# A sine on a constant: from the last place of ScalarE's order to its first

## The chip, the cores and the metric

The kernel runs on 1 core of one Trainium2 chip. The metric is device time in microseconds (us) of one execution. Three runs of the kernel before took 228.07, 229.65 and 228.75 us; their median, 228.75, is the time before.

Engines are named as in the profile: PE is TensorE, DVE is VectorE, ACT is ScalarE, POOL is GpSimd, SP is SyncE. "L591" is line 591 of the kernel's file.

## The reference

An attention with sketched features feeds a mixing block. There are 4 batches, 4 heads, 1088 tokens, head dimension 32, and 8 rows in each sketch; the model dimension is 128.

```python
def phi(x):                                   # 8 x 8 = 64 features
    a = np.einsum('rd,bhsd->bhsr', S1, x)
    b = np.einsum('rd,bhsd->bhsr', S2, x)
    return np.einsum('bhsi,bhsj->bhsij', a, b).reshape(*x.shape[:-1], r * r)
q_p, k_p = (phi(q), phi(k))
kv = np.einsum('bhsf,bhsd->bhfd', k_p, v)
z = np.sum(k_p, axis=2)
attn = np.einsum('bhsf,bhfd->bhsd', q_p, kv) / (np.einsum('bhsf,bhf->bhs', q_p, z)[..., None] + 1e-06)
x = attn.transpose(0, 2, 1, 3).reshape(B, S, H * D)      # (4, 1088, 128)
theta = x @ w_theta
zr, zi = x * np.cos(theta), x * np.sin(theta)
y = np.einsum('ts,bsd->btd', w_tok_r, zr) + np.einsum('ts,bsd->btd', w_tok_i, zi)
u = x + y
out = u + np.maximum(u @ w_ch, 0.0)
```

The token mixing, two 1088 x 1088 matrices on four batches, is the largest part of the work.

## The kernel before

**A list of operations with a written order.** The program doesn't issue instructions as it goes through its loops. It calls `op(engine, duration, function, writes, reads)` for each step, which notes the step in a list with the steps that it depends on; the engine is a letter (P for PE, V for DVE, A for ACT, G for POOL, S for SP), and the duration is used only where orders are planned. Then three tables written into the file decide the rest: `SEQUENCE` is the order in which all 1024 steps are issued, `PLACES` gives each of the 419 buffers its slot (a stretch of SBUF of a class such as "big" or "zs", or a PSUM bank), and `FILLS` puts 6 filler matmuls ahead of one small transpose (L418). Each engine works through its own steps in that order. Where two buffers share a slot, the first writer of the later one waits for the last reader of the earlier one, so a change in `PLACES` alone can make or remove waits.

**The opening.** POOL clears a small tile (L368), PE runs 11 filler matmuls and then the 6 of `FILLS` on it (both L366), DVE writes the constants (L347 to L361), among them `halfpi`, a column with pi/2 (L348), which the cosine takes as its bias (L1048). SP loads the two sketches into `st` (L381, L382), after DVE has cleared it (L388); ACT and DVE turn their words into fp32 (L395, L407), and PE transposes two maxima (L418). In the meantime k and q come in (L611, L649).

**The weights.** All inputs come as 8-byte words. `w_tok` is cut into 17 blocks of 128 x 1088 words, numbered 0 to 16. For each, `weight()` has SP load the words into a "zs" slot (L587); ACT makes the upper words into fp32 with a Prelu (L591, in two halves) and copies the lower words' bits into a "big" slot, the "step" (L594); DVE shifts the first (L315), and the sum of both is made either by a DVE instruction (L311) or, for the blocks 3, 5, 7 and 9 to 16, by a transfer that POOL issues and that adds into its target (`join`, L325). SP's next load of `w_tok` waits until ACT has read the words in the slot that it takes.

**Attention and angles.** Per batch, PE makes products of features and values, DVE their numerators and ACT copies them between (L986, L1091, L1100). `theta_stage` (L1019) has PE compute theta (L331) and turn x (L1035) for three chunks at a time; ACT rounds (L1044), DVE takes the difference (L318), ACT takes its absolute value (L1047), then the cosine as a sine with the bias `halfpi` (L1048) and the sine (L1050); DVE multiplies with x (L311).

**Mixing.** Batches are taken in the pairs (0, 1) and (2, 3), with fewer large products than the plain sum has. Many are sums of PE products over blocks of `w_tok` (L331), with POOL transfers or DVE making sums of the blocks themselves. `early_products` (L1302) copies a first product out of PSUM on ACT (L1314), which frees the bank for PE's next one; `carried` (L1324) scales it (L1333) and adds it back by POOL transfers. The last steps are the channel mix, the maximum, and the output transfers from SP.

**The sine on a constant.** The kernel's fourth step (L371) computes a sine of `halfpi` into a tile `warm` that nothing reads. In `SEQUENCE` it stands at the end of ACT's order. ACT's functions come in tables that an instruction loads (ACT_TABLE_LOAD in the profile); these loads aren't written in the kernel's file, they are put in when it is built, where a function needs another table than the one before it.

Of the kernel before, what the change touches and what calls it, by code (L numbers as in the profile page):

```python
# [17 lines left out]
AF = mybir.ActivationFunctionType  # L18
# [28 lines left out]
    0, 4, 5, 6, 2, 1, 7, 8, 10, 11, 9, 30, 89, 49, 95, 101, 31, 12, 13, 35, 52, 53, 90, 76, 50, 14, 15, 233, 20,  # L47
    91, 92, 102, 51, 290, 55, 56, 57, 58, 214, 54, 34, 59, 60, 77, 16, 96, 93, 236, 61, 62, 63, 64, 65, 66, 67,
    68, 78, 238, 17, 182, 36, 69, 215, 70, 71, 185, 239, 159, 187, 72, 73, 241, 242, 183, 184, 237, 240, 74, 33,
    160, 161, 131, 75, 80, 81, 26, 37, 134, 294, 27, 28, 132, 136, 234, 235, 300, 21, 82, 83, 292, 79, 295, 291,  # L50
    293, 296, 97, 98, 99, 29, 163, 84, 164, 139, 140, 243, 141, 210, 162, 301, 85, 86, 220, 221, 124, 133, 125,
    87, 142, 143, 175, 144, 244, 176, 103, 245, 104, 297, 216, 177, 88, 217, 135, 105, 18, 190, 191, 138, 19,
    178, 22, 145, 246, 322, 192, 193, 194, 302, 303, 427, 247, 109, 428, 325, 211, 137, 298, 299, 188, 304, 324,
    431, 432, 423, 424, 425, 212, 248, 305, 429, 430, 426, 186, 195, 433, 434, 435, 196, 169, 170, 118, 197,
    198, 213, 165, 166, 306, 323, 42, 44, 249, 250, 108, 251, 307, 334, 252, 253, 254, 255, 310, 311, 146, 147,
    148, 149, 436, 189, 167, 437, 326, 335, 226, 308, 227, 150, 151, 438, 439, 309, 312, 256, 152, 257, 258,
    153, 119, 154, 259, 440, 171, 43, 45, 32, 336, 23, 260, 155, 156, 157, 94, 100, 106, 337, 222, 441, 442, 46,
    199, 200, 201, 47, 48, 346, 348, 443, 202, 203, 204, 347, 107, 349, 110, 364, 444, 205, 206, 269, 445, 158,
    270, 366, 207, 313, 208, 448, 449, 446, 447, 365, 24, 209, 38, 452, 265, 111, 453, 454, 266, 228, 267, 455,
    268, 456, 112, 229, 459, 350, 172, 223, 271, 457, 179, 261, 458, 460, 272, 462, 475, 340, 341, 40, 352, 342,  # L60
    327, 450, 273, 477, 173, 274, 275, 338, 368, 276, 382, 168, 174, 277, 343, 351, 451, 467, 354, 478, 461,
    180, 367, 369, 353, 113, 355, 469, 470, 677, 385, 476, 673, 230, 463, 471, 181, 678, 679, 356, 328, 680,
    329, 278, 472, 224, 357, 262, 344, 473, 283, 464, 345, 468, 41, 669, 670, 671, 672, 674, 675, 676, 114, 115,
    339, 474, 492, 218, 681, 465, 466, 483, 314, 682, 683, 479, 481, 358, 263, 684, 282, 685, 480, 485, 486,
    219, 225, 360, 686, 316, 605, 264, 361, 494, 315, 482, 359, 120, 330, 284, 496, 287, 231, 687, 688, 370,
    371, 121, 317, 487, 318, 484, 319, 495, 285, 489, 689, 690, 691, 694, 705, 692, 698, 488, 320, 116, 695,
    232, 373, 394, 497, 525, 279, 693, 491, 490, 372, 529, 530, 531, 532, 521, 522, 523, 524, 122, 526, 527,
    528, 332, 696, 697, 39, 117, 331, 533, 534, 535, 536, 537, 708, 709, 288, 538, 396, 286, 699, 700, 706, 25,
    707, 539, 540, 541, 397, 126, 127, 128, 602, 701, 702, 499, 710, 711, 542, 557, 395, 333, 703, 704, 412,
    415, 384, 607, 713, 715, 123, 543, 129, 130, 721, 716, 560, 723, 604, 280, 561, 558, 559, 413, 493, 281,  # L70
    546, 547, 544, 545, 289, 550, 714, 717, 724, 321, 383, 603, 562, 563, 548, 549, 600, 553, 722, 554, 386,
    414, 416, 387, 718, 729, 731, 719, 720, 823, 824, 362, 551, 363, 388, 827, 828, 829, 552, 555, 725, 831,
    832, 833, 727, 400, 726, 728, 398, 399, 825, 830, 417, 556, 564, 374, 375, 391, 739, 834, 826, 740, 835,
    732, 565, 390, 389, 392, 393, 733, 734, 401, 735, 743, 738, 584, 606, 836, 837, 730, 838, 736, 376, 377,
    498, 576, 578, 579, 742, 585, 402, 839, 840, 841, 842, 567, 378, 737, 741, 575, 744, 380, 580, 500, 501,
    745, 746, 502, 843, 844, 418, 587, 588, 506, 504, 747, 629, 748, 752, 750, 577, 849, 847, 505, 404, 379,
    755, 848, 569, 845, 751, 846, 509, 582, 586, 381, 503, 581, 403, 589, 749, 590, 570, 419, 566, 405, 850,
    851, 591, 593, 592, 583, 596, 571, 572, 573, 599, 595, 420, 852, 421, 631, 598, 422, 853, 601, 854, 855,
    856, 857, 568, 507, 753, 612, 611, 406, 624, 613, 574, 594, 597, 610, 407, 756, 408, 410, 626, 770, 409,
    869, 871, 872, 614, 619, 646, 860, 862, 873, 609, 615, 874, 608, 878, 411, 510, 875, 617, 616, 508, 653,  # L80
    618, 645, 649, 623, 754, 712, 858, 868, 620, 511, 870, 863, 651, 880, 881, 876, 882, 884, 888, 647, 512,
    627, 656, 758, 877, 879, 859, 861, 655, 625, 652, 893, 635, 621, 622, 634, 769, 864, 866, 757, 767, 771,
    785, 778, 883, 886, 772, 768, 891, 650, 885, 777, 628, 774, 865, 867, 636, 887, 779, 633, 889, 931, 787,
    788, 637, 638, 639, 890, 897, 640, 641, 632, 643, 784, 780, 892, 648, 644, 630, 898, 773, 903, 654, 789,
    657, 659, 915, 775, 917, 786, 759, 658, 782, 660, 642, 760, 513, 900, 916, 761, 776, 514, 904, 515, 516,
    762, 790, 783, 792, 791, 805, 804, 914, 930, 806, 793, 795, 920, 929, 919, 896, 794, 796, 895, 800, 901,
    797, 661, 908, 662, 899, 909, 808, 963, 911, 807, 801, 802, 924, 798, 918, 902, 985, 811, 781, 913, 3, 810,
    907, 905, 812, 809, 814, 906, 813, 984, 965, 517, 518, 519, 932, 938, 520, 665, 666, 925, 663, 962, 667,
    819, 923, 799, 934, 763, 820, 821, 910, 935, 936, 912, 803, 960, 922, 921, 939, 926, 894, 927, 955, 937,
    933, 961, 940, 964, 967, 764, 928, 941, 765, 957, 952, 953, 942, 943, 946, 956, 966, 944, 822, 947, 948,  # L90
    959, 954, 958, 968, 998, 815, 668, 766, 986, 983, 969, 664, 949, 816, 817, 951, 989, 971, 973, 945, 950,
    970, 994, 972, 988, 818, 995, 978, 979, 980, 990, 981, 974, 975, 987, 1000, 976, 992, 999, 1004, 977, 982,
    1009, 1003, 1001, 1006, 1012, 1013, 991, 1008, 1014, 1015, 1007, 1002, 1005, 1011, 993, 997, 996, 1010,
    1020, 1021, 1022, 1023, 1016, 1017, 1018, 1019,
# [3 lines left out]
    46, 57, 47, 45, 60, 49, 56, 46, 54, 53, 47, 57, 57, 39, 61, 50, 34, 58, 40, 56, 50, 35, 59, 41, 61, 48, 36,  # L98
    52, 45, 62, 48, 60, 59, 44, 62, 46, 36, 56, 42, 57, 49, 37, 62, 43, 59, 54, 38, 45, 53, 31, 12, 16, 55, 58,
    41, 52, 9, 61, 62, 15, 62, 44, 62, 37, 60, 41, 61, 34, 55, 40, 62, 35, 54, 51, 30, 7, 19, 58, 55, 39, 51,  # L100
    14, 56, 61, 60, 42, 57, 36, 57, 39, 60, 35, 60, 40, 56, 34, 29, 49, 29, 5, 10, 58, 59, 44, 50, 5, 60, 53,
    54, 51, 46, 47, 49, 62, 52, 45, 60, 46, 57, 47, 49, 51, 53, 52, 59, 53, 45, 56, 48, 51, 62, 41, 62, 60, 56,
    32, 60, 61, 57, 33, 61, 62, 57, 28, 56, 60, 59, 32, 18, 22, 17, 19, 25, 1, 0, 24, 2, 10, 22, 12, 8, 25, 4,
    16, 23, 1, 4, 26, 14, 6, 26, 21, 2, 23, 21, 7, 23, 11, 9, 24, 7, 1, 26, 14, 12, 26, 11, 21, 24, 5, 5, 26,
    11, 17, 23, 3, 3, 26, 11, 27, 61, 62, 57, 20, 50, 13, 22, 38, 34, 59, 56, 61, 35, 36, 57, 58, 57, 38, 36,
    55, 58, 56, 20, 61, 61, 37, 59, 56, 38, 60, 57, 37, 55, 58, 31, 55, 41, 58, 39, 27, 62, 56, 61, 17, 50, 20,
    24, 36, 34, 60, 56, 56, 36, 38, 56, 62, 56, 34, 38, 60, 56, 59, 1, 59, 57, 38, 44, 61, 61, 36, 39, 60, 59,
    35, 40, 57, 60, 55, 58, 28, 62, 43, 60, 41, 27, 58, 57, 55, 17, 53, 15, 25, 36, 35, 59, 56, 59, 34, 36, 57,
    61, 56, 38, 35, 56, 61, 57, 11, 61, 61, 35, 60, 57, 37, 60, 57, 34, 62, 56, 30, 57, 40, 60, 39, 56, 62, 62,
    44, 56, 42, 60, 58, 57, 40, 58, 40, 27, 59, 62, 61, 5, 46, 14, 23, 23, 34, 34, 37, 59, 57, 60, 61, 5, 61,  # L110
    59, 37, 39, 55, 61, 34, 42, 59, 61, 35, 43, 26, 59, 61, 33, 57, 55, 57, 44, 60, 42, 58, 62, 57, 39, 60, 41,
    56, 55, 61, 62, 43, 58, 44, 59, 42,
)
FILLS = (
    (11, 6),
)


class Buf:


    def __init__(self, cls, shape, dt, name):
# [11 lines left out]
class Layout:  # L134
# [11 lines left out]
    def op(self, eng, dur, fn, w=(), r=(), acc=(), hold=(), lk=0, kind=0, mode=0, n=1, fly=0.0):  # L146
        o = Op()
# [11 lines left out]
        for x in r:  # L159
            b, key = parts(x)  # L160
# [1352 lines left out]
```

## Time and profile before

| what | value |
|---|---|
| runs | 228.07, 229.65, 228.75 us; median 228.75 |
| the profiled execution's own time | 229.23 us |
| its span, first to last instruction | 227.4 us (1.83 us of its time lie around the span) |
| mean granted clock of TensorE | 0.992 |
| ACT_TABLE_LOAD | 2 times, 1.28 us each: before the first L395 and before the first L1048 |
| sines L1048 | 12 times, 0.60 to 0.68 us |
| transfers of w_tok | 17, of 1088 KB, median 9.6 us from issue to landing |
| POOL's transfers that add | 44 of L325, 4.1 to 16.4 us from issue to landing |

A line of the timeline has the start in us, the duration in us, the engine, the line, the operation, the tiles (output<-input) with their shape, and how many instructions are put together; in brackets stands how long the engine was idle before and what ended that wait. In the chain of work, followed back from the last instruction, a line is one piece with its start, its length, and what it was. The windows give the busy time of each engine in a stretch.

### The profile page before, as it was taken

The numbers are of one execution on the slowest core, as the hardware profiler recorded it, in microseconds if no ns is written. First come the engines' busy times: TensorE is split into PE (matmuls) and PEld (weight loads), VectorE is DVE, ScalarE is ACT, GpSimd is POOL, SyncE is SP. The second block draws the span as 40 slices with busy tenths as digits, with TensorE's granted clock in tenths as the row PEclk, the third lists the DMA queues.
The fourth block names the chain that finished last, engine by engine and source line by source line (L and its number), as shares of the span: only waits on it lengthen the run. The fifth ranks groups of instructions, "written<-read, shape, count | busy, mean of one in ns | idle before, by whom it ended". The sixth has DMA issues, their size and how long they took to land.

```text
span 227.4 us, 4055 instructions
## 1 busy us (share of the span) xinstructions
PE 217.8 (96%) x1486; PEld 182.2 (80%) x1486; DVE 171.0 (75%) x388; ACT 126.1 (55%) x260; POOL 55.2 (24%) x92
## 2 busy tenths in 40 slices
PE   7999999998979999899989999999999999999993
PEld 3898999976867886588868788888888888888882
DVE  2799999999999989789997917985483663504763
ACT  2988798999999997999997545730000000000000
POOL 1067960001116300013322361968000000000000
PEclk9999999999979999999999999999999999999999
DMA  4999999994999999299999899999973000331442
GB/s 130 421 420 312 383 353 417 419 425 147 246 299 188 299 257 273 89 291 242 275 243 207 255 191 167 176 191 194 198 128 52 0 0 3 62 58 23 69 74 58
DMA packets 28888, 46.80 MB, mean 206 GB/s; under 512 B 18757, under 2 KB 19013, under 8 KB 26693
## 3 DMA queue, kind: packets, MB, share of 16 engines
q1 hardware_dynamic: 22532, 30.30, 39.0%
q0 software_dynamic: 6336, 16.26, 37.3%
q8 instruction: 11, 0.18, 0.3%
q14 instruction: 9, 0.07, 0.1%
HBM read 28.07 MB, written 2.23 MB: 133 GB/s over the span
## 4 chain that ended last, share of the span: by engine, by line
PE 54%; DVE 24%; DMA 10%; ACT 7%; issue 3%; POOL 0%; SPq 0%; DVEq 0%; ACTq 0%; POOLq 0%
PE ps L331 49%; DMA big<-big 5%; DVE big L311 5%; DMA zs<-w_tok 4%; DVE g L311 3%; DVE sm L318 2%; PE ps L366 2%; DVE hf L315 2%; DVE big L315 2%; DVE sm L311 2%; ACT big L591 2%; PE ps L1035 1%; DVE sm L315 1%; DVE lv L311 1%; PE ps L1087 1%
## 5 line engine op out<-in xcount | busy, mean ns | idle before, releaser
L331 PE MATMUL ps<-big,zs 128*128 128x288 f32 (+2 forms) x498 | 116.2, 387 | 2.2 <-DVE zs L311 1.4
L331 PEld LDWEIGHTS ps<-big,zs 128*128 128x128 f32 x498 | 91.2, 191 | 20.5 <-DVE zs L311 1.5
L325 POOL DMA_DIRECT2D big<-big x35 | 33.5, 1347 | 89.9 <-DVE big L315 29.7
L591 ACT ACTIVATE big<-zs 128x544 f32<-128x544 f32 (+1 forms) x33 | 23.3, 727 | 0.7 <-DMA zs<-w_tok 0.7
L594 ACT ACTIVATE big<-zs 128x1088 int32<-128x1088 uint32 (+1 forms) x18 | 21.4, 1190 | 3.1 <-DMA big<-big 1.7
L318 DVE SCALAR_TENSOR_TENSOR big<-ps,even,big 128x288 f32<-128x288 f32 (+2 forms) x23 | 10.5, 483 | 16.1 <-PE ps L331 15.8
L331 PE MATMUL ps<-mf,big 128*128 128x96 f32 x72 | 14.5, 295 | 0.1
L311 DVE TENSOR_TENSOR zs<-ps,g 128x768 f32<-128x768 f32 (+2 forms) x20 | 12.5, 630 | 2.1 <-ACT g L1050 1.7
L315 DVE TENSOR_SCALAR big<-big 128x1088 int32<-128x1088 int32 x17 | 12.2, 725 | 1.3 <-ACT big L591 1.1
L331 PEld LDWEIGHTS <-hf 128*128 128x128 f16 (+1 forms) x144 | 11.9, 105 | 1.2 <-issue 0.8
L311 DVE TENSOR_TENSOR big<-big,ps 128x288 f32<-128x288 f32 (+1 forms) x12 | 5.1, 433 | 9.9 <-PE ps L331 9.8
L311 DVE TENSOR_TENSOR g<-lv 128x768 f32<-128x768 f32 x12 | 11.2, 952 | 1.4 <-PE ps L1087 1.2
L331 PE MATMUL ps<-w,big 128*128 128x128 f32 (+1 forms) x76 | 12.2, 299 | 0.0
L331 PEld LDWEIGHTS ps<-w,big 128*128 128x128 f32 x76 | 10.7, 202 | 1.8 <-PE ps L331 0.6
L318 DVE SCALAR_TENSOR_TENSOR big<-ps,big 128x288 f32<-128x288 f32 (+1 forms) x15 | 6.5, 434 | 6.6 <-PE ps L331 6.5
L331 PEld LDWEIGHTS ps<-mf,big 128*128 128x128 f32 x72 | 10.9, 191 | 0.4 <-issue 0.4
L311 DVE TENSOR_TENSOR big<-big,hf 128x1152 f32<-128x1152 f32 x8 | 11.0, 1385 | 0.0
L325 POOL DMA_DIRECT2D big<-hf x9 | 10.3, 1300 | 2.8 <-DVE sm L315 2.0
L331 PE MATMUL ps<-mv,hf 128*128 128x96 f16 x108 | 10.8, 206 | 0.1
L331 PE MATMUL ps<-big,big 128*128 128x128 f32 x72 | 10.9, 279 | 0.0
L331 PE MATMUL ps<-sbk,g 128*128 128x64 f32 x72 | 9.5, 272 | 0.0
L331 PEld LDWEIGHTS ps<-big,big 128*128 128x128 f32 x72 | 9.3, 192 | 0.1
(195 smaller groups left out, 381.0 us busy)
## 6 DMA issues: line engine op xcount, KB each, us to landing
zs<-w_tok SPq DMA_DIRECT2D x17, 1088.0 KB, 9.6
big<-big POOLq DMA_DIRECT2D x24, 272.0 KB, 8.7
big<-big POOLq DMA_DIRECT2D x11, 544.0 KB, 9.1
big<-k_l SPq DMA_DIRECT2D x7, 576.0 KB, 7.6
big<-q_l SPq DMA_DIRECT2D x4, 576.0 KB, 6.6
big<-v_l SPq DMA_DIRECT2D x4, 576.0 KB, 9.1
big<-hf POOLq DMA_DIRECT2D x3, 576.0 KB, 10.1
big<-hf POOLq DMA_DIRECT2D x6, 272.0 KB, 10.9
```

Source lines behind the costliest of these rows:

```text
L311: eng.tensor_tensor(out=o, in0=a, in1=b, op=f)
L315: (eng or V).tensor_scalar(out=o, in0=a, scalar1=s1, scalar2=s2, op0=op0, **kw)
L318: (eng or V).scalar_tensor_tensor(out=o, in0=a, scalar=s, in1=b, op0=op0, op1=op1)
L325: op("G", n * 2.55e-3, lambda: G.dma_start(dst(), src(), accum_op=ALU.add), w, r, kind=2)
L331: T.matmul(o, lhs, rhs, start=start, stop=stop, skip_group_check=True)
L366: T.matmul(nowhere() if out is None else out, idle()[:, 0:P], idle(), start=True, stop=True, skip_group_check=True)
L591: op("A", 0.19 + (c1 - c0) * 0.0009, lambda c0=c0, c1=c1, scale=scale, alpha=alpha: A.activation(dfn()[:, c0:c1], words_of(raw(), n)[1][:, ...
L594: op("A", 0.22 + n * 0.0009, lambda: A.activation(stp(), words_of(raw(), n)[0].bitcast(U32), AF.Copy, scale=2.0**-29), [stp], [raw])
L1035: T.transpose(x()[:, i], xs()[:, off + i * P:off + (i + 1) * P], ident())
L1087: T.transpose(tr()[:, i * P:(i + 1) * P], qp()[:, i * H + 2 * n:i * H + 2 * n + 2].rearrange("p h i j -> p (h i j)"), ident())
```

## The change

The step on the constant moves, and its operand is written first:

- `halfpi` is written by a DVE step of its own, ahead of the other constants (and so ahead of the clearing of `st`).
- the sine of `halfpi` stands at the front of ACT's order instead of at its end. All other steps keep their order on every engine; the numbers in `SEQUENCE` and `FILLS` are one higher because there is one step more.
- with it the program has one table load, at the very front of ACT, before the first sine; the load ahead of the first L395 and the one ahead of the first L1048 are gone. The sine at the end is gone from there.
- `PLACES` differs in 77 of its 419 numbers. Eight are "big" slots: block 9 of `w_tok` goes from slot 7 to 21 and block 13 from slot 21 to 7; block 11's step and five other buffers trade slots 5 and 14. The other 69 are PSUM banks among 56 to 62 that products trade. Through the first of these, the wait for POOL's adding transfer of block 10 (it reads the step that lies in slot 7 before) moves on ACT from block 9's first L591 to block 13's first L591, which stands three instructions ahead of it.
- `leader` makes the first ACT step a predecessor of all later ones, and `blocks_again` gets a longer duration; both only matter where orders are planned.

The core of the diff, in which the tables are cut:

```diff
 SEQUENCE = (
-    0, 4, 5, 6, 2, 1, 7, 8, 10, 11, 9, 30, 89, 49, 95, 101, 31, 12, 13, 35, 52, 53, 90, 76, 50, 14, 15, 233, 20,
+    2, 4, 0, 5, 6, 7, 3, 1, 8, 9, 11, 12, 10, 31, 90, 50, 96, 102, 32, 13, 14, 36, 53, 54, 91, 77, 51, 15, 16,
...
-    16, 23, 1, 4, 26, 14, 6, 26, 21, 2, 23, 21, 7, 23, 11, 9, 24, 7, 1, 26, 14, 12, 26, 11, 21, 24, 5, 5, 26,
+    16, 23, 1, 4, 26, 14, 6, 26, 21, 2, 23, 21, 21, 23, 11, 9, 24, 7, 1, 26, 5, 12, 26, 11, 7, 24, 14, 14, 26,
...
 FILLS = (
-    (11, 6),
+    (12, 6),
 )
...
+        self.leader = []
...
+        if eng == "A":
+            pred.update(self.leader)
+            self.leader = self.leader or [o.i]
...
     def constants():
-        V.memset(halfpi(), math.pi / 2.0)
         V.memset(ups()[:, 0:1], 2.0**14)
...
-    op("V", 1.5, constants, [hm, bdm, halfpi, ups, ones, grids], [])
-    op("A", 0.3, lambda: A.activation(warm(), halfpi(), AF.Sin), [warm], [halfpi])
+    op("V", 0.1, lambda: V.memset(halfpi(), math.pi / 2.0), [halfpi], [])
+    op("V", 1.5, constants, [hm, bdm, ups, ones, grids], [])
+    op("A", 1.5, lambda: A.activation(warm(), halfpi(), AF.Sin), [warm], [halfpi])
...
     for b in range(1, B):
-        op("G", 1.2, lambda b=b: blocks_again(b), [(mv[b], "s"), (mf[b], "s")], [(mv[0], "s"), (mf[0], "s")], lk=3)
+        op("G", 2.2, lambda b=b: blocks_again(b), [(mv[b], "s"), (mf[b], "s")], [(mv[0], "s"), (mf[0], "s")], lk=3)
```

## The prediction

> **What bounds the kernel now.** I read the page first (busy times, chain), then ScalarE's timeline around both table loads, then the chain in order of time from 50 to 160 us, then the waits behind it.
>
> ```profile
> PE 217.8 (96%) x1486; PEld 182.2 (80%) x1486; DVE 171.0 (75%) x388; ACT 126.1 (55%) x260; POOL 55.2 (24%) x92
> PE 54%; DVE 24%; DMA 10%; ACT 7%; issue 3%; POOL 0%; SPq 0%; DVEq 0%; ACTq 0%; POOLq 0%
> ```
>
> TensorE is the bound. ScalarE, whose order changes, works 55% of the span and holds 7% of the chain. So a microsecond taken from ScalarE is worth one only where PE, VectorE or a transfer then starts earlier.
>
> The two loads that the change touches, in ScalarE's timeline:
>
> ```profile
> 3.37 1.28 ACT L395 ACT_TABLE_LOAD   x1 [3.37 <-DMA st<-s]
> 4.67 0.24 ACT L395 ACTIVATE sp<-st 128x48 f32<-128x48 f32 x1
> ...
> 6.12 1.16 ACT L633 ACTIVATE big<-big 128x1152 f32<-128x1152 f32 x1 [0.16 <-DMA big<-k_l]
> ...
> 60.41 0.72 ACT L591 ACTIVATE big<-zs 128x544 f32<-128x544 f32 x1
> 61.13 1.28 ACT L1048 ACT_TABLE_LOAD   x1
> 62.43 0.61 ACT L1048 ACTIVATE g<-g,halfpi 128x384 f32<-128x384 f32 x1
> ```
>
> The chain in order of time, first its opening, then the middle:
>
> ```profile
> 1.34 5.62 PE ps L366 x17
> 6.96 0.22 PE ps L418
> ```
>
> ```profile
> 79.10 0.46 ACT g L1091
> 79.56 0.61 ACT big L591
> 80.19 9.44 DMA zs<-w_tok
> ...
> 107.23 0.65 DVE big L315
> 107.88 0.28 issue
> 108.16 11.32 DMA big<-big
> 119.48 0.04 issue
> 119.52 3.93 PE ps L331 x16
> ```
>
> The reader should see that the opening is 17 filler matmuls, and that two transfers, of 9.44 and 11.32 us, carry the middle.
>
> **The change part by part.**
>
> *First load.* It moves from 3.37 (behind the landing of st) to the front of ScalarE, about 0.8 us, when VectorE's first memsets run (halfpi at 0.90). Load 1.28 and the new sine (0.24 as L395, a short one) end near 2.4, before st lands at 3.37. So L395 can run 1.3 us earlier, and VectorE's small chain behind it. The gain is 0: the small transpose L418 stands behind the fillers, which end at 6.96, and ScalarE's own next long work, L633 at 6.12, waits for k. Cover gone, it would be -1.3. Against it: halfpi's memset (0.06) now stands ahead of st's, which SP's L381 at 0.98 waits for; +0.06 at most, under the same fillers. SP's queue keeps its order. I take 0, ends 0 and +0.06.
>
> *Second load.* L591 starts at 60.41 and L1048 at 62.43. A row of L591's form is followed after 0.61 to 0.62 (68.76 to 69.37, 108.91 to 109.53), so the load costs 2.02 - 0.61 = 1.41 us of ScalarE.
> The page "ScalarE: Activation LUTs" of the Trainium skill, section "What ACT_TABLE_LOAD costs", puts 1283 ns of load and 1380 ns of drain on every switch, 2.66 us. The trace has the 1283 but only 0.13 more; by the Trainium skill's figure this term would be 2.66 where I have 1.41, and what passes the next lines would be the same 0.4.
>
> Where do the 1.41 us survive? At 68.39 L1044 reads a product that PE ended at 67.91: at most 0.48 passes. PE got there from VectorE (its 1.40 idle at 64.72 waits for DVE's L311), and VectorE waits for ScalarE nowhere between 57 and 81.6. At 75.75 PE's L1087 turns a VectorE product that is done about 0.35 earlier; ScalarE's L1091 at 76.28 had 0.02 of slack against PE. So about 0.4 is left when L591 (79.46) frees the slot for the w_tok transfer of 80.19. Other ScalarE work at 81.04, 81.85, 86.73 and 87.76 starts 0.02 behind PE, so it moves only with PE. What is late next is that transfer:
>
> ```profile
> 80.00:90.00 10.00, 10.00 (x93) 7.51 (x92) 8.83 (x18) 8.34 (x17) 0.00 (x0) 1.00 1.00 248
> ```
>
> That row of the windows (the last three columns are clock, DMA share, GB/s) has all 16 DMA engines busy; the v_l transfer ahead in SP's queue lands only at 81.30, and POOL's last join shares the engines to 89.83. An issue 0.4 earlier stands longer in line: 0 to -0.4 at 89.63. I take 0, since v_l's landing, not the issue, starts that service. ScalarE waits 1.42 there, so its whole order behind is anchored on the landing.
>
> *The last sine goes* from the end of ScalarE, where nothing waits for it: 0.
>
> *New places.* Two results of L591 exchange slots 7 and 21. Block 13's (107.39) now lies where block 10's low words lie, and these are still read by POOL's accumulating transfer of 98.20, which lands at 108.89. Before, it was block 9's L591 that waited for it, at 108.91, 0.02 behind the landing.
>
> ```profile
> 106.86 0.61 ACT L1048 ACTIVATE g<-g,halfpi 128x384 f32<-128x384 f32 x1
> 107.39 0.71 ACT L591 ACTIVATE big<-zs 128x544 f32<-128x544 f32 x1
> 107.99 0.51 ACT L1050 ACTIVATE g<-g 128x384 f32<-128x384 f32 x1
> 108.40 0.60 ACT L1027 ACTIVATE g<-big,even 128x384 f32<-128x384 f32 x1
> 108.91 0.71 ACT L591 ACTIVATE big<-zs 128x544 f32<-128x544 f32 x1
> ```
>
> ScalarE stops at 107.39 until 108.91: +1.52 us, and the whole order behind it shifts. The sine L1050 ends at 110.03 instead of 108.51, just as VectorE needs it (110.03). VectorE's L318 (110.63) gets L1044's result at 111.5: +0.9, which its idle 1.10 at 123.88 takes back. PE's matmul at 112.52 had its bank freed by the copy L1314 at 112.41, 0.11 before: PE starts 1.1 to 1.4 later. Then:
>
> ```profile
> 119.52 3.93 PE L331 MATMUL ps<-big,zs 128*128 128x288 f32 x16 [0.80 <-DMA big<-big]
> ```
>
> PE stands 0.80 here for the join issued at 108.16. VectorE's L315 that releases it ends at 107.88, before anything is late, so its landing at 119.48 stays and takes 0.80 of the delay: 0.3 to 0.6 remain. Next is the join of block 9: its L594 (114.11) comes 1.1 later, its issue goes from 115.67 to about 116.8. POOL's queue served its joins one behind the other: those of full size landed 2.6 to 2.7 us after the landing ahead of them (116.87 to 119.48, 120.84 to 123.52, 123.52 to 126.15; a half-sized one came in at 120.84). Block 9's service starts at 120.84 whether issued at 115.67 or 116.8: its landing stays, and so do block 13's and the carry's behind it. PE, 0.04 behind that landing at 123.56, gets back part of the rest. I take +0.2 at the end (the residue of 0.3 less what small gaps return), ends 0 and +1.3 (the larger delay at 112.52, nothing absorbed but the 0.11).
>
> Smaller: L594 at 102.89 moves to a slot whose last reader on PE ends at 102.3: 0, cover 0.6; without it, +0.6 on ScalarE. PSUM banks trade places among products seven or more program steps apart: 0, ends -0.1 and +0.1. POOL's own waits for block 10's landing move from block 9's join (115.67) to block 13's (119.09), both after 108.89: 0.
>
> *Sum.* 0 + 0 + 0 + 0.2. The profiled execution took 229.23 (span 227.4 and 1.83 around it), so 229.43; it stands 0.48 above the median 228.75, so 228.95, said as 228.9.
>
> **The rivals.**
>
> A. *The load's time reaches the end.* For it: the load is on the chain, and so are 79.56 and 80.19. Against: the 0.48 at 68.39, the saturated engines. If shorter queues also move 71.78's transfer, up to 1.41 passes 89.63, and the new stop at 107.39 must then be hidden too: 228.75 - 1.41 = 227.35.
> By the figure of the Trainium skill (the same page and section) A would give 226.1; the trace's own rows leave no room for a second 1.3 us between 60.41 and 62.43.
>
> B. *The new wait decides (slower).* Place: L591 at 107.39 behind the landing of 108.89. Price: 1.1 us at PE's 112.52. It decides if joins keep their time from issue to landing (block 9: 7.85 us) rather than their place in POOL's queue; then block 9 lands at 124.6, PE at 123.56 waits 1.1, and PE is busy from there to 221. Time 228.75 + 1.1 = 229.85. Against it: the equal steps of 2.6 us.
>
> C. *The early set doesn't serve the other functions*, and a load stays. Against it: after 62.43 the same L591, L594, L1044 and L1143 forms run at their old lengths with no load, in the sine's set. If it stayed at 61.13, only the new wait is left: 228.95 still, and up to 229.85 with B.
>
> **How the numbers follow.** Chances: forecast 0.60, A 0.14, B 0.21, C 0.03, 0.02 for something unseen. The likeliest is 228.9. The range goes from A (227.35, said as 227.4) to B's upper bound, the whole stop of 1.52 at the end: 230.27, said as 230.3. It leaves out A or B with a further mishap (0.11 in all, below) and some 0.05 for the spread of the runs (228.07 to 229.65). The forecast's own range is 228.35 (the -0.4) to 229.4. A measurement of this kernel tells about 1% (2.3 us) from no change; A at 227.35 and B at 229.85 are both inside it. Faster by over 1% needs A and, with it, PE's clock dip gone (the windows show 0.72 granted from 65 to 71, 0.28 x 6 = 1.7 us): 225.6, 0.05. Slower by over 1% needs B and a dip of that size elsewhere: 231.5, 0.06. Within 1%: 0.89.
>
> **What would show it.** Right: one load, at the front, none before L1048; PE's L418 still near 6.9; w_tok's transfer of 80.19 issued about 0.4 earlier and landing within 0.4 of 89.63; ScalarE idle 1 to 1.5 us at the L591 near 107.4, released by a big<-big transfer; PE's idle near 119.5 down from 0.80 to under 0.2; block 9 landing near 123.5. Wrong: PE ahead by over 0.6 at 90 to 100 (A); block 9 landing over 0.8 later, with PE waiting (B); a second load (C).

## The result, and the profile after

The changed kernel takes 230.94 us (median of 6 runs, 230.31 to 233.86) against 228.78 us (6 runs, 228.07 to 229.65): a ratio of 1.0084, 95% interval 1.0056 to 1.0111. A second set, taken beside the experiments, gave 230.24 us against 229.05 and 1.0038 (1.0012 to 1.0063). So the change makes the kernel slower, by 0.4% in one set and 0.8% in the other. (Times are medians of all runs; the ratios leave out runs over 1.5% above the fastest of the same kernel.) Forecast were 228.9 us and a range that ended at 230.3.

The profiled execution of the changed kernel took 230.31 us (span 228.4). In code and profile of the changed kernel line numbers are 3 to 4 higher: L335 is L331 of before, L595 is L591, L1052 is L1048. The page's two lines:

```profile
PE 216.6 (95%) x1486; PEld 180.2 (79%) x1486; DVE 171.3 (75%) x388; ACT 124.9 (55%) x259; POOL 55.3 (24%) x92
PE 46%; DVE 30%; DMA 13%; issue 4%; ACT 4%; POOL 2%; SPq 0%; POOLq 0%; DVEq 0%; ACTq 0%
```

ScalarE is 1.2 us less busy, and its share of the chain fell from 7% to 4%. But TensorE's fell too, from 54% to 46%: the chain now runs through more waits, for transfers above all (10% to 13%). ScalarE's timeline shows that the change did what it says:

```profile
0.72 1.28 ACT L375 ACT_TABLE_LOAD   x1 [0.72 <-PEq L1507]
2.01 0.20 ACT L375 ACTIVATE warm<-halfpi 128x1 f32<-128x1 f32 x1
3.43 0.25 ACT L399 ACTIVATE sp<-st 128x48 f32<-128x48 f32 x1 [1.22 <-DMA st<-s]
...
60.17 0.72 ACT L595 ACTIVATE big<-zs 128x544 f32<-128x544 f32 x1
60.79 0.61 ACT L1052 ACTIVATE g<-g,halfpi 128x384 f32<-128x384 f32 x1
...
107.62 0.72 ACT L595 ACTIVATE big<-zs 128x544 f32<-128x544 f32 x1 [1.37 <-DMA big<-big]
```

One load, at the front and hidden; at 60.17 the sine follows L595 after 0.62 us where it took 2.02. And ScalarE stands 1.37 us at block 13, as forecast. Where this goes on TensorE, two stretches of PE's timeline show:

```profile
112.67 5.77 PE L335 MATMUL ps<-big,zs 128*128 128x288 f32 x24 [1.00 <-ACT hf L1318]
118.28 0.49 PE L1039 MATMUL ps<-ident,g 128*128 128x128 f32 x3
118.61 3.83 PE L335 MATMUL ps<-big,zs 128*128 128x288 f32 x16
...
139.19 1.08 PE L335 MATMUL ps<-big,zs 128*128 128x288 f32 x4
141.48 1.40 PE L335 MATMUL ps<-big,zs 128*128 128x288 f32 x5 [1.21 <-DMA big<-big]
```

All but 0.2 us of what is lost at 112.67 is had back at 118.61, where before had stood 0.80 idle. The second idle time, 1.21 us at 141.48, was in no forecast. In the kernel before, PE ran through this place:

```profile
139.31 0.83 PE L331 MATMUL ps<-w,big 128*128 128x128 f32 x6
139.98 3.40 PE L331 MATMUL ps<-big,zs 128*128 128x288 f32 x14
```

Set side by side, the same matmuls are 1.02 us ahead of before at 120 and 0.79 ahead at 139, and 0.58 behind at 140.9. The loss lies between the last two. (Part of that lead is due to the profile shown of before, whose clock was at half for 3.41 us from 65.0. The changed kernel's second profile, experiment 5, has such a half clock too; it is 0.30 ahead at 139 and 0.61 behind at 141.1. So the two spans, 227.4 and 228.4, differ by less than the times.)

What is late at 141.48 is an adding transfer that POOL issues at 133.95. The chain says so, and the windows say how:

```profile
133.95 7.39 DMA big<-big
141.35 0.14 issue
141.48 3.91 PE ps L335 x16
```

```profile
138.00:140.00 2.00, 2.00 (x14) 1.66 (x12) 1.27 (x3) 0.00 (x0) 0.00 (x0) 1.00 1.02 188
140.00:142.00 2.00, 0.79 (x4) 0.49 (x3) 0.66 (x2) 0.63 (x1) 0.12 (x1) 1.00 0.18 32
```

The DMA share (next to last column) drops from 1.02 to 0.18 while PE still waits: nearly all DMA engines had finished, and one had not. The transfer lands in sixteen shares, as many as the page counts DMA engines, and the records of their landings say the same: fifteen landed from 139.06 to 139.43, the last at 141.35. The trace's packets don't tell their engine, but one of them fits: a piece of instructions, 16 KB in one packet, started at 136.88 and took 1.65 us. The page counts these packets in its queue q8 (11 over the span, 0.18 MB, the same in both kernels):

```profile
q8 instruction: 11, 0.18, 0.3%
```

In the kernel before, the piece came at 141.69, when the same transfer had landed (140.46 for the fifteenth share, 140.56 for the last). Below, a "hit" is such a piece falling on this transfer, with its last share late and PE idle behind it, and "the wait" is ScalarE's new one at block 13.

### The profile page after: what moved, and what is told of

Read it like the earlier page. It is cut to its first block, busy times and chain, and to the rows that moved or that the text cites. A ratio compares the mean times of both kernels' runs of the same rounds, so it can differ in the third digit from the quotient of the medians.

```text
span 228.4 us, 4057 instructions
## 1 busy us (share of the span) xinstructions
PE 216.6 (95%) x1486; PEld 180.2 (79%) x1486; DVE 171.3 (75%) x388; ACT 124.9 (55%) x259; POOL 55.3 (24%) x92
## 4 chain that ended last, share of the span: by engine, by line
PE 46%; DVE 30%; DMA 13%; issue 4%; ACT 4%; POOL 2%; SPq 0%; POOLq 0%; DVEq 0%; ACTq 0%
PE ps L335 42%; DMA big<-big 8%; DVE big L315 5%; DVE g L315 5%; DMA zs<-w_tok 4%; DVE big L319 3%; DVE sm L322 3%; DVE hf L319 2%; DVE lv L315 2%; DVE zs L315 2%; PE ps L369 2%; DVE sm L315 2%; POOL big L329 2%; DVE sm L319 2%; ACT big L595 1%
## 5 line engine op out<-in xcount | busy, mean ns | idle before, releaser
L335 PE MATMUL ps<-big,zs 128*128 128x288 f32 (+2 forms) x498 | 116.2, 386 | 3.9 <-DVE zs L315 1.7
L335 PEld LDWEIGHTS ps<-big,zs 128*128 128x128 f32 x498 | 90.6, 190 | 23.0 <-DVE zs L315 2.0
L595 ACT ACTIVATE big<-zs 128x544 f32<-128x544 f32 (+1 forms) x33 | 23.3, 723 | 2.7 <-DMA big<-big 1.4
L335 PE MATMUL ps<-mf,big 128*128 128x96 f32 x72 | 14.5, 295 | 0.1
L335 PEld LDWEIGHTS <-hf 128*128 128x128 f16 (+1 forms) x144 | 11.9, 105 | 1.2 <-issue 0.8
L335 PE MATMUL ps<-w,big 128*128 128x128 f32 (+1 forms) x76 | 11.5, 287 | 0.0
L335 PEld LDWEIGHTS ps<-w,big 128*128 128x128 f32 x76 | 10.0, 191 | 1.7 <-PE ps L335 0.6
L335 PEld LDWEIGHTS ps<-mf,big 128*128 128x128 f32 x72 | 10.9, 191 | 0.4 <-issue 0.4
L335 PE MATMUL ps<-mv,hf 128*128 128x96 f16 x108 | 10.8, 206 | 0.1
L335 PE MATMUL ps<-big,big 128*128 128x128 f32 x72 | 10.8, 277 | 0.0
L335 PE MATMUL ps<-sbk,g 128*128 128x64 f32 x72 | 9.6, 274 | 0.2 <-DVE g L322 0.2
L335 PE MATMUL ps<-g,big 128*64 128x128 f32 x144 | 9.4, 277 | 0.2 <-DMA big<-v_l 0.2
```

What stands on the lines that cost most here:

```text
L335: T.matmul(o, lhs, rhs, start=start, stop=stop, skip_group_check=True)
L595: op("A", 0.19 + (c1 - c0) * 0.0009, lambda c0=c0, c1=c1, scale=scale, alpha=alpha: A.activation(dfn()[:, c0:c1], words_of(raw(), n)[1][:, ...
```

## The experiments

Three theories, and a fourth that came with the second set:
- F: TensorE's own instruction fetch. The new places bring PE three more semaphore instructions (48 before, 51 after, counted in the trace); these shift the piece that PE fetches next from 141.7 to 136.9 us, onto the transfer that PE waits for.
- W: ScalarE's new wait at block 13 (the forecast's rival B).
- S: the early sine itself, through all that then moves.
- P: the traded places cost by their own waits on PE, and the fetch is only a bystander.

Every kernel was timed in 5 rounds, 12 runs of each, beside runs of the kernel before on the same chip. In experiments 3, 4, 6, 9 and 10 the file is a line shorter, so their line numbers are one lower.

**1. The sine first, with the places of before.** The edit puts the old table `PLACES` into the changed kernel.

> The changed kernel with the places of before: the sine stands first and there is one table load, but no buffer changes its slot. ScalarE has no wait for block 10's join ahead of block 13, and PE has three semaphore instructions fewer than the changed kernel (as before). Theory F (PE's own instruction fetch, 16 KB on one DMA engine, comes in at 136.9 us instead of 141.7 and holds up the last sixteenth of the join that PE waits for at 141.4): no such hit here, fetch after 140, last landing within 0.6 us of the first; time 0.3 to 1.0 us under before, 227.8 to 228.5. Theory W (ScalarE's new wait at block 13 is what costs): also no cost, the same time. Theory S (the earlier front itself makes the kernel slower, wherever transfers then fall): 229.8 to 231, as the changed kernel.

Measured: 228.68 us, ratio 0.9981 (0.9954 to 1.0007). Fetch at 141.06, transfer whole at 139.97, no idle time near 140. S falls: the early sine alone isn't slower.

**2. The order of before, with the new places.** The edit puts the new table into the kernel before.

> The kernel before with the places of the change: two table loads, the sine last, ScalarE's new wait at block 13, and three more semaphore instructions on PE. Theory F: PE's fetch near 137 hits the join, its last sixteenth lands about 1.9 us behind the others, PE idle 1.2 to 2 us near 141; 1.2 to 2.2 us over before, 230.0 to 231.0. Theory W: 1.1 us over before at PE's matmul near 112.5, and at the end 229.5 to 230.0. Theory S: no cost from places, 228.3 to 229.3.

Measured: 230.63 us, ratio 1.0055 (1.0033 to 1.0076). Fetch at 137.94, last share at 141.75 (fifteenth 140.39), PE idle 0.87 us. The places carry the loss, and bring it without the sine.

**3. The changed kernel without the wait at block 13.**

```diff
-    16, 23, 1, 4, 26, 14, 6, 26, 21, 2, 23, 21, 21, 23, 11, 9, 24, 7, 1, 26, 5, 12, 26, 11, 7, 24, 14, 14, 26,
+    16, 23, 1, 4, 26, 14, 6, 26, 21, 2, 23, 21, 7, 23, 11, 9, 24, 7, 1, 26, 5, 12, 26, 11, 21, 24, 14, 14, 26,
```

> The changed kernel with slots 7 and 21 exchanged back for blocks 9 and 13, nothing else: ScalarE's new wait is gone, PE's three more semaphore instructions stay. Theory F: still slow, the fetch near 136.5 to 137 and PE idle 1.2 to 2 us near 141; 230.0 to 231.2. Theory W: the cost is gone, 228.0 to 228.9. Theory S: as the changed kernel, 230.3 to 231.2.

Measured: 229.31 us, ratio 1.0005 (0.9977 to 1.0032). A miss for F's size and inside nobody's range: fetch at 136.69, last share at 140.14 (fifteenth 139.25), PE idle 0.49. The hit is there, and the median is 0.6 us above experiment 1's, not the 1.2 that F expected; the two intervals overlap, so these times alone don't prove a loss.

**4. The sine first and the wait at block 13, the other places as before.**

```diff
-    16, 23, 1, 4, 26, 14, 6, 26, 21, 2, 23, 21, 7, 23, 11, 9, 24, 7, 1, 26, 14, 12, 26, 11, 21, 24, 5, 5, 26,
+    16, 23, 1, 4, 26, 14, 6, 26, 21, 2, 23, 21, 21, 23, 11, 9, 24, 7, 1, 26, 14, 12, 26, 11, 7, 24, 5, 5, 26,
```

> The sine first with the places of before, but slots 7 and 21 exchanged for blocks 9 and 13: ScalarE's new wait is there, PE's three more semaphore instructions are not. Theory F: fetch after 140, no hit; ScalarE stands 1.1 to 1.5 us at block 13, PE loses it at 112.6 and has it back at 119.5; 228.0 to 228.9. Theory W: 1.1 to 2 us over before, 229.8 to 230.9. Theory S: 230.3 to 231.2.

Measured: 228.63 us, ratio 0.9984 (0.9957 to 1.0010), the same as without the wait. PE's timeline has the idle time at 112 and nothing at 118 or 140:

```profile
112.24 5.77 PE L334 MATMUL ps<-big,zs 128*128 128x288 f32 x24 [0.90 <-ACT hf L1317]
117.85 0.49 PE L1038 MATMUL ps<-ident,g 128*128 128x128 f32 x3
118.17 2.00 PE L334 MATMUL ps<-big,zs 128*128 128x288 f32 x8
...
138.73 4.07 PE L334 MATMUL ps<-big,zs 128*128 128x288 f32 x17
```

W falls as a cause by itself.

**5. The changed kernel once more.**

> The changed kernel once more, for a second profile and for times beside the next three. Theory F (PE's fetch hits the join it waits for): fetch between 136 and 138, last sixteenth of that join 0.9 to 2 us behind the others, PE idle 0.5 to 1.3 us near 141; 230 to 231. Theory P (the traded banks cost by their own waits on PE, not by the fetch): the same time, but the idle time near 141 may stand elsewhere. Theory C (the loss is chance of single runs): 228.7 to 229.7.

Measured: 230.24 us, ratio 1.0038 (1.0012 to 1.0063). Fetch at 137.74, last share at 141.30 (fifteenth 140.30), PE idle 0.68. Not chance of single runs.

**6. Experiment 4 with four more PE instructions.** One filler matmul of 384 columns becomes three of 128; no place, wait or bank changes.

```diff
-    def spin(out=None):
-        T.matmul(nowhere() if out is None else out, idle()[:, 0:P], idle(), start=True, stop=True, skip_group_check=True)
+    def spin(out=None, w=GW):
+        T.matmul(nowhere()[:, :w] if out is None else out, idle()[:, 0:P], idle()[:, :w], start=True, stop=True, skip_group_check=True)
...
-    span = [op("P", 3.2, lambda: [spin() for _ in range(11)], [nowhere], [idle])]
+    span = [op("P", 3.2, lambda: [spin() for _ in range(10)] + [spin(w=P) for _ in range(3)], [nowhere], [idle])]
```

> The sine first, old places but for slots 7 and 21 (as e5), and one of the first eleven filler matmuls cut into three of 128 columns: same columns, two matmuls and two weight loads more on PE, no bank or wait changed. Theory F: all of PE's later fetches move four instructions ahead, the one of 146.1 goes to 136 to 138 and hits the join; PE idle 0.5 to 1.3 us near 140, 1.0 to 2.0 us slower than e5, 229.7 to 230.7. Theory P: as e5, 228.3 to 229.0, fetch past 140.

Measured: 229.87 us, ratio 1.0039 (0.9999 to 1.0079), against 0.9984 of experiment 4. The fetch went from 146.10 to 136.67 and made the hit. PE's timeline, chain and windows have the mark of the changed kernel:

```profile
138.66 1.08 PE L334 MATMUL ps<-big,zs 128*128 128x288 f32 x4
140.53 2.31 PE L334 MATMUL ps<-big,zs 128*128 128x288 f32 x9 [0.79 <-DMA big<-big]
```

```profile
133.39 7.01 DMA big<-big
140.40 0.14 issue
140.53 3.90 PE ps L334 x16
```

```profile
138.00:140.00 2.00, 1.74 (x11) 1.23 (x9) 1.77 (x4) 0.00 (x0) 0.00 (x0) 1.00 0.98 182
140.00:142.00 2.00, 1.47 (x6) 1.25 (x7) 0.43 (x2) 1.26 (x2) 1.07 (x2) 1.00 0.06 10
```

**7. The changed kernel with four fewer PE instructions.** Eight filler matmuls of 384 columns become six of 512; all places and all three semaphore instructions stay.

```diff
-    nowhere = buf("ps", (GW,), F32, "nowhere")
+    nowhere = buf("ps", (4 * P,), F32, "nowhere")
-    def spin(out=None):
-        T.matmul(nowhere() if out is None else out, idle()[:, 0:P], idle(), start=True, stop=True, skip_group_check=True)
+    def spin(out=None, wide=False):
+        rhs = bc(idle()[:, 0:P], 1, [P, 4, P]) if wide else idle()
+        T.matmul((nowhere() if wide else nowhere()[:, :GW]) if out is None else out, idle()[:, 0:P], rhs, start=True, stop=True, skip_group_check=True)
...
-    span = [op("P", 3.2, lambda: [spin() for _ in range(11)], [nowhere], [idle])]
+    span = [op("P", 3.2, lambda: [spin() for _ in range(3)] + [spin(wide=True) for _ in range(6)], [nowhere], [idle])]
```

> The changed kernel with eight of the filler matmuls (384 columns) replaced by six of 512: same columns, two matmuls and two weight loads fewer on PE; the banks, the three semaphore instructions and ScalarE's wait all stay. Theory F: the fetch goes back past 140, no sixteenth is late, no PE idle near 141; 1.2 to 2.2 us faster than the changed kernel beside it, 228.4 to 229.2. Theory P: as the changed kernel, 230 to 231.

Measured: 229.13 us, ratio 0.9992 (0.9964 to 1.0019); fetch at 141.99. Its profiled execution, at 232.05 us, shows something else: PE stood 1.98 us idle at 134.3, behind an adding transfer whose fifteenth share landed at 131.95 and whose last at 134.26. The w_tok transfer ahead of it (129.06 and 131.57) and the next three of POOL's were 2.0 to 2.5 us late in their last share too, and no piece of instructions was fetched meanwhile: the last one had ended at 124.98, before the first packet of these transfers. So a late share has another cause as well, which stays open. The kernel was run again.

> The changed kernel with four PE instructions fewer in the opening once more, for a profile without the 1.98 us idle at 134.3 that the first one had. Theory F: fetch past 140, no late sixteenth, no PE idle near 141, within 0.2% of before, 0.4% under the changed kernel. Theory P: 0.4% over before.

Measured: 228.42 us, ratio 0.9977 (0.9948 to 1.0005); fetch at 140.13, transfer whole at 139.07, no idle time:

```profile
138.67 4.07 PE L335 MATMUL ps<-big,zs 128*128 128x288 f32 x17
```

The chain of this execution has PE alone from 126.50 for 16.68 us, where the changed kernel's has 7.39 us of transfer. With every place of the change still in it, the kernel is 0.5% to 0.6% faster than the changed one in experiment 5. P falls.

**8. The kernel before, with four more PE instructions.** The edit of experiment 6, in the kernel before.

> The kernel before, nothing of the change in it, with one filler matmul of the opening cut into three of 128 columns: two matmuls and two weight loads more on PE. Theory F (PE's instruction fetch hits the join that PE waits for): fetch near 137.5 instead of 141.7, last sixteenth of the join about 1 us late, PE idle 0.5 to 1 us near 141.5; 0.4 to 0.6% over before (1.0 to 1.4 us). Theory P (the traded banks or the early sine cost, not the fetch): within 0.2% of before.

Measured: 229.67 us, ratio 1.0020 (0.9998 to 1.0042). Fetch at 136.97, last share at 140.70 (fifteenth 139.49), PE idle 0.69:

```profile
139.06 1.08 PE L331 MATMUL ps<-big,zs 128*128 128x288 f32 x4
140.83 1.86 PE L331 MATMUL ps<-big,zs 128*128 128x288 f32 x7 [0.69 <-DMA big<-big]
```

The mechanism is as F expects, in a kernel with nothing of the change in it; its size, 0.55 us in the medians and just inside the noise, is half of what F expected, as in experiment 3.

**9. The changed kernel with slots 5 and 14 as before.** PE then has one more semaphore instruction than before (49).

```diff
-    16, 23, 1, 4, 26, 14, 6, 26, 21, 2, 23, 21, 21, 23, 11, 9, 24, 7, 1, 26, 5, 12, 26, 11, 7, 24, 14, 14, 26,
+    16, 23, 1, 4, 26, 14, 6, 26, 21, 2, 23, 21, 21, 23, 11, 9, 24, 7, 1, 26, 14, 12, 26, 11, 7, 24, 5, 5, 26,
...
```

> The changed kernel with slots 5 and 14 as before and the rest of its places: ScalarE's wait at block 13 stays, of PE's three more semaphore instructions one stays. Theory F: this finds the border: either the fetch is past 140 (no idle near 141, within 0.3% of before) or near 137 (0.3 to 0.6% over). Theory P: 0.3 to 0.8% over before, wherever the fetch is.

Measured: 230.94 us, ratio 1.0063 (1.0031 to 1.0095). Fetch at 136.24, last share at 140.44 (fifteenth 139.39), PE idle 0.75. One more instruction is enough.

**10. The kernel before with the wait at block 13 alone.** The edit of experiment 4, in the kernel before.

> The kernel before with slots 7 and 21 exchanged for blocks 9 and 13 and nothing else: ScalarE's new wait without the sine in front and without a changed number of PE instructions. Theory F (the wait is harmless by itself, since PE takes back near 119.5 what it loses near 112.5; it costs only together with PE's fetch hitting a join): fetch past 140, PE idle 0.8 to 1 us near 113 in place of 0.8 near 119.5, within 0.2% of before. Theory W (the wait costs by itself): 0.3 to 0.5% over before.

Measured: 229.28 us, ratio 1.0004 (0.9975 to 1.0032); fetch at 146.54, PE idle 0.64 at 112.64 and none near 140. W falls here as well.

**11. Experiment 1 with 34 more PE instructions.** All 17 filler matmuls are cut into halves of 192 columns; `spin` is changed as in experiment 6.

```diff
...
-    span = [op("P", 3.2, lambda: [spin() for _ in range(11)], [nowhere], [idle])]
+    span = [op("P", 3.2, lambda: [spin(w=GW // 2) for _ in range(22)], [nowhere], [idle])]
...
-        L.issue(pools, spin)
+        L.issue(pools, lambda: [spin(w=GW // 2) for _ in range(2)])
```

> The sine first with the places of before (as e1), and all 17 filler matmuls cut into two halves: same columns, 34 more PE instructions. Theory F: fetches move some 3 to 4 us ahead: the ninth to about 133.5, done before the join that lands near 139.9 is served, so no idle near 140 over 0.3; the seventh from 104.7 to about 101. Time as e1, 228.2 to 229.2; faster if the seventh no longer makes the joins from 106 to 126 late by 1 us (227.5). Theory P: as e1.

Measured: 230.08 us, ratio 1.0016 (0.9991 to 1.0041); both theories had expected experiment 1's time. The profiled execution took 238.77 us with TensorE's clock at half for 20.48 us from 17.8, so its times can't be set beside the others'. But it has a hit: the piece started at 142.68, just behind the transfer's issue at 142.40, the last share landed at 149.24 (fifteenth 148.23), and PE stood 0.59 us idle. F had expected that an earlier piece would be done before the transfer is served; it wasn't.

All profiles but the first of 7 and that of 11, in the order of PE's instructions beyond those of before; the transfer is the one of about 134 us, with its fifteenth and its last share, and "both" marks wait and hit:

```
kernel                 PE instr.  wait at 13  fetch at  took   15th    16th    PE idle  ratio
7b four fewer             -1        yes       140.13    1.27   138.92  139.07   0       0.9977
before                     0        no        141.69    1.29   140.46  140.56   0       1
1  sine, old places        0        no        141.06    1.41   139.85  139.97   0       0.9981
4  sine, wait              0        yes       146.10    0.94   138.89  139.12   0       0.9984
10 before, wait            0        yes       146.54    0.90   139.36  139.50   0       1.0004
9  one semaphore          +1        yes       136.24    1.46   139.39  140.44   0.75    1.0063  both
3  change, no wait        +3        no        136.69    1.04   139.25  140.14   0.49    1.0005
2  old order, places      +3        yes       137.94    1.18   140.39  141.75   0.87    1.0055  both
   changed kernel         +3        yes       136.88    1.65   139.43  141.35   1.21    1.0084  both
5  changed, again         +3        yes       137.74    1.14   140.30  141.30   0.68    1.0038  both
8  before, four more      +4        no        136.97    1.06   139.49  140.70   0.69    1.0020
6  sine, wait, four more  +4        yes       136.67    0.89   139.19  140.40   0.79    1.0039  both
```

The border lies between 0 and +1: with no more PE instructions than before the piece comes after 140 us, when the transfer has landed; with one more it comes at 136 to 138, and a share of that transfer is 0.9 to 1.9 us late, every time.

What a hit costs can be read from the stretch of PE's work across it, the same matmuls in every kernel (138.18 to 143.22 in before). It takes 5.04 us in all six profiles without the hit, the first of experiment 7 among them, and 5.77 to 6.49 us in the eight with it (6.49 in the changed kernel, 5.87 in experiment 11): 0.7 to 1.5 us lost. From there to PE's last matmul every profile takes 80.5 to 80.9 us, so nothing is had back and nothing more is lost.

The page "DMA: Bandwidth & Descriptors" of the Trainium skill, section "Queues, rings and completion order", says that each DMA engine goes round between the queues that have work for it, packet by packet, and finishes a packet before it changes. The traces fit this: a 16 KB piece is one packet of 0.9 to 1.65 us, and only one share of sixteen is late.

## Why the prediction was wrong

*First load: right.* It ran at 0.72 to 2.00 and L399 waited for st as before; PE's small transpose stood at 6.44 instead of 6.75, behind the fillers.

*Second load: its size right, its survival too small.* The load cost 2.02 - 0.62 = 1.40 us (forecast 1.41). The Trainium skill's 2.66 us for a switch ("ScalarE: Activation LUTs", "What ACT_TABLE_LOAD costs") isn't seen here: what came free is the load's 1.28 and 0.12 more. But of it I let 0.4 us pass to the w_tok transfer and none to its landing. Experiments 10 and 4 differ only in the sine's place, and neither profile has the half clock at 65: the transfer was issued at 79.38 and 78.60, landed at 88.71 and 88.06, and the spans are 226.9 and 226.2. So 0.78 us passed, and 0.65 of it arrived. With the half clock in both (before and experiment 1) 0.27 passed, the landing came 0.40 earlier, and the spans are 227.4 and 226.9. These are single profiles. Two things failed. The slack of 0.48 at 68.39 was read from an execution whose PE had been slowed by the half clock just there; without it PE waits for ScalarE, as experiment 10 shows:

```profile
70.42 0.33 PE L910 MATMUL ps<-ident,sm 128*128 128x128 f32 x1 [0.39 <-ACT big L955]
73.64 0.55 PE L1034 MATMUL ps<-ident,big 128*128 128x128 f32 x3 [0.69 <-ACT big L955]
```

And the landing followed the issue, though the engines were full. The three kernels with the early sine and no hit, one of them timed twice, have 0.9977 to 0.9992; each interval holds 1, so a gain of 0.2 to 0.5 us is likely, not proven, where I had +0.2 for the whole change. The sign that I had set for rival A, PE ahead by over 0.6 at 90 to 100, is there in the first profile (1.1 to 1.2); in experiment 5, whose profile has the half clock of before, PE is only 0.05 to 0.3 ahead.

*New wait on ScalarE: right.* 1.37 us at block 13 (forecast 1.52), 1.00 at PE's 112.67 (forecast 1.1 to 1.4), taken back but for 0.2 by the idle 0.80 near 119.5; block 9 landed at 122.25, not later than before. Experiments 4 and 10 put its price without the hit at nothing that could be measured. Rival B had the right sign and the wrong place.

*PSUM banks and the step's slot: the step that failed.* I wrote "PSUM banks trade places ... 0, ends -0.1 and +0.1" and "L594 at 102.89 moves to a slot ... 0". As waits they cost nothing (experiment 7, with all of them in it, is no slower than before). But they brought PE three semaphore instructions, one by the banks and two by the slots 5 and 14 (49 and 51, experiment 9), and these moved a fetch 4 us ahead, onto the transfer that PE needed next. I had counted what the moved places wait for, not what instructions the waits add. What the runs show in place of 0: 0.7 to 1.5 us in the profiles, and in the medians 0.5 to 0.6 us where ScalarE's wait is missing (experiments 8 and 3 against before and 1, neither clear of noise alone), about 0.5%, or 1.1 to 1.2 us, where it is there (6 against 4, 5 against 7).

*What stays open.* In the medians the hit costs more with the wait than without it: 0.5% to 0.8% (6 against 4, 5 against 7, 9 against 4) and 0.2% (8 against before, 3 against 1). The profiles show less of a difference: 0.9 to 1.45 us lost at the place in the five measurements marked "both", 0.7 and 0.9 in the two with the hit alone. Half of the runs of those five that count in the ratios had a mean granted clock below 0.995 (23 of 46), against 22 of 79 in the other seven (the two of experiment 7 among them, without 11). Among runs from that clock up the hit costs about the same with the wait (6 against 4: 229.26 and 228.56) and without (3 against 1: 229.19 and 228.47; 8 against before: 229.65 and 229.06), but 1.0 us in 5 against 7 (229.64 and 228.65) and 1.35 in 2 against before (230.45 and 229.10), so the clock isn't all of it. That more idle time on PE makes half clock more frequent was only argued: where the clock fell in runs without a trace isn't known. It may also be why the changed kernel was measured at 1.0084 and at 1.0038.

Why one instruction moves the fetch by 4 us is not shown either. PE's rows for semaphore instructions give a hint. In before, experiment 1 and both profiles of 7 the piece starts 1.0 to 1.1 us behind the start of the row that waits for this very transfer (140.58 in before); in 4 and 10 it comes behind a later row; in the changed kernel it starts 4.5 us ahead of that same row (141.38). A stream of instructions whose next piece is due just behind such a row, or just ahead of it, would do this.

## What to carry to other kernels

A change of places, orders or waits also changes how many instructions an engine has, and so when its next piece of instructions is fetched: look in the trace for the instruction packets, and for transfers of which one share in sixteen lands late just then. A late share alone is not enough, as the first profile of experiment 7 shows. Four instructions more or fewer, in matmuls that do nothing, made such a hit and undid it here, and told it from the places' own waits. And before reading slack from a profile, look at the clock of that stretch: 0.27 of the load's 1.40 us passed on with a half clock of 3.4 us there, and 0.78 without it.

## What the runs showed of the hardware

- PE's instructions come in pieces of 16 KB, 11 within the span and one behind it in the two kernels' profiles, each one packet of 0.9 to 1.65 us. That they are PE's is inferred from experiments 6 to 8, which change PE's instructions alone and move the piece; that they take up a DMA engine that data needs too, from the one late share. An engine may stay behind while all are full: in the kernel before, every one of POOL's transfers that landed from 108.9 to 127.5, behind the piece of 105.22, was 1 us or more late in its last share (117.38 to 118.45 for fifteen shares and 119.48 for the last one, of the transfer issued at 108.16), and PE's 0.80 idle at 119.52 is such a last share. That the piece did this is likely, but no run shows it.
- TensorE's clock fell to half for 3.41 us just behind an idle time of PE of 1.4 us (64.72) in the profiles of before and of experiments 1, 2 and 5, and not in the others, which have the same idle time; in the first profile of experiment 7 it did so at 135.1, behind 1.98 us idle. With the fillers cut in halves (experiment 11) it was at half for 20.48 us from 17.8 in the profiled execution, and 3 of the 12 runs had a mean clock of 0.946 to 0.957:

```profile
18.00:38.00 20.00, 20.00 (x116) 19.70 (x117) 13.56 (x34) 10.26 (x23) 8.25 (x28) 0.50 1.03 355
```
